# High parts of the differences one step behind their sums, and early differences in scratch in the order of use

## The chip, the cores and the metric

The kernel runs on one core of a Trainium2 chip. The metric is the device time of one execution in microseconds, as the median of several runs. The engines are TensorE (PE in the profile; PEld is its weight load), VectorE (DVE), ScalarE (ACT), GpSimdE (POOL) and SyncE (SP), which here only issues DMAs. Each engine takes its instructions in the order of the program and waits at an instruction until what it needs is there.

## The reference

```python
x = A_x                                   # 1 x 2048 x 640
xn = layernorm(x)
# A: 32 heads of 20, each position attends to 8 positions at distance 0, 2, ..., 14 behind it
q, k, v = split(xn @ wqkv)
o = sum_w softmax_w(q . k[s - 2w] * scale) * v[s - 2w]
s = o @ wo
# B: bilinear GLU, F = 1536
g = silu(((xn @ w_gate) * (xn @ w_up)) @ w_down)
out = x + s * g
```

## The kernel before

All products run on TensorE in a form that splits each fp32 operand into a high and a low part and takes three products (high x high, high x low, low x high): `ALL3`. A high part is a ScalarE copy into the float32r type, a low part is the GpSimdE or VectorE difference of the raw value and the high part.

The normalised, transposed input `xT` lies in SBUF in four chunks of 512 positions (buffers `xc`), each with high and low parts. The gate and up products of the GLU take two chunks at a time with a seven-product scheme (function `group`, line 1296 for its matmuls): of each pair of chunks it needs, beside the blocks themselves, the differences T1, T2, T3, T4 for two rows k = 0, 1 of the blocks. For the first pair of chunks (0 and 1) they are made early (`early_sums`, `early_high`), stored to a scratch in HBM, `t_scr`, of 12 units of 128 x 512, and loaded again by `load_t(n)`, three units at a time, into four SBUF tiles: load 0 is issued near the end of the qkv stage, loads 1 to 3 in the first `group` of the second pair. All are issued on GpSimdE's queue (line 1152). `T2_UNIT` gives the place of each difference in the scratch. For the second pair (chunks 2 and 3) the generator `differences(k)` makes them in SBUF while the qkv products run: `sums` is one GpSimdE addition or subtraction (line 1166), `parts` is one ScalarE copy (high part, line 1170) and one GpSimdE subtraction (low part, line 1171). T4 is kept raw until `last_difference`.

The order on each engine is the order in which the code issues. In the qkv stage (the loop over m and t from line 1360 on) each step issues one product of fifteen matmuls (`qkv`, line 435), its ScalarE copy out of PSUM (line 449), a DMA of every second copy to HBM scratch (line 453), a piece of attention (`advance`; lines 497 to 579, with GpSimdE's sums in line 515), at some steps a split of the next weights (lines 115 and 117), and, by a rate, one step of `differences`. So `yield` in `differences` is where other work comes between.

The PSUM banks of the qkv products in this stage are taken in turn: `ring[:] = [q_one, "g", "u"]`, where `q_one` is a single bank, and g and u have two each. In `group`, the seven products are issued in this order, which the names in the change refer to:

```python
W_IN = ("B11", "T1", "T2", "B22", "T3", "B21", "T4")
for n, j in enumerate((0, 5, 2, 1, 4, 3, 6)):
    y = b["ACACABA"[j]]
    runs = [(w_unit(f, H_IN[j], k)[i], x_in(W_IN[j], l, k, c0)) for i, l in ALL3 for k in range(2)]
```

So the order of use is B11, B21, T2, T1, T3, B22, T4, and within each first the high parts of k = 0, 1 and then the low parts.

Of the kernel before, what the change touches and what calls it, by code (L numbers as in the profile page):

```python
# [56 lines left out]
def kernel(  # L57
# [25 lines left out]
    def st(shape, tag, bufs, dt=F32):  # L83
        cnt[0] += 1
        pool = sb
        if tag == "gh":
            pool, bufs = gh_pool
        return pool.tile(shape, dt, tag=tag, bufs=bufs, name=f"{tag}_{cnt[0]}")
# [523 lines left out]
    def early_high(k):  # L612

        r0, r1, a, b = early_t[:4]
        for n, (j, y) in enumerate((("T1", a), ("T2", b), ("T3", r0), ("T4", r1))):
# [3 lines left out]
            for l, t in enumerate((early_t[4 + n], y)):  # L619
                nc.sync.dma_start(t_scr[:, T2_UNIT[j, l] + k] if j != "T4" else e_scr[l][:, k], t)  # L620

    T2_UNIT = {(j, a): 2 * n for n, (j, a) in enumerate((j, a) for j in ("T1", "T2", "T3") for a in range(2))}

    def advance(budget):
        credit[0] += budget
# [514 lines left out]
    def t_unit(j, a, k, c0=2):  # L1140

        if j == "T4":
            return xT[c0 + 1][a][:, k, :]
        n, i = T_UNIT[j, a, k] if c0 else divmod(T2_UNIT[j, a] + k, 3)
        while len(tt[c0]) <= n:
            tt[c0].append(slot([P, 3, CH]))
        return tt[c0][n][:, i]
# [12 lines left out]
    def differences(k):  # L1160

        def x(ch, a, m):
            return xT[ch][a][:, 2 * m + k, :].bitcast(F32)

        def sums(out, u, v, eng=nc.gpsimd.tensor_sub):
            eng(out, u, v)
            yield

        def parts(j, y):
            nc.scalar.activation(t_unit(j, 0, k), y, AF.Copy)  # L1170
            nc.gpsimd.tensor_sub(t_unit(j, 1, k), y, t_unit(j, 0, k).bitcast(F32))
            yield

        r0, a = st([P, CH], "gh", 5), st([P, CH], "gh", 5)
        yield from sums(r0, x(3, 0, 0), x(3, 1, 0), nc.gpsimd.tensor_add)
        yield from sums(a, r0, x(2, 0, 0))
        yield from sums(a, a, x(2, 1, 0))
        yield from parts("T1", a)
        r1 = st([P, CH], "gh", 5)
        yield from sums(r1, x(3, 0, 1), x(3, 1, 1), nc.gpsimd.tensor_add)  # L1180
        yield from sums(r0, r1, r0)
        yield from parts("T3", r0)
        yield from sums(r1, r1, a)
        yield from parts("T2", r1)
        z = t4[k] = st([P, CH], "gh", 5)
        yield from sums(z, x(2, 0, 1), r1)
        yield from sums(z, z, x(2, 1, 1), nc.gpsimd.tensor_add)

    def last_difference(k):
# [158 lines left out]
    def first_parts():  # L1348
# [4 lines left out]
        yield  # L1353

    steps += [differences(k) for k in range(2)]
    paced = 0.0
    last, BLOCK = len(MADE) - 1, (3, 4, 6, 8, 10)
    W_SUMS = ((1, 12), (2, 4), (2, 12), (3, 7))
    RATE = ((1.0, 0.4), (0.3, 0.2), (0.4, 0.6), (0.8, 0.8))
    for m, t in ((m, t) for m in range(1, len(MADE)) for t in range(DIL)):  # L1360
# [3 lines left out]
        for i in range(NE):  # L1364
            n = t * NE + i
# [185 lines left out]
    for m in range(n_prod):  # L1551
        n, j = divmod(m, 7)
# [82 lines left out]
```

## Time and profile before

| | |
|---|---|
| median of 3 runs | 739.09 us (739.0 to 740.01) |
| the profiled execution | 737.8 us, its span 736.0 us |
| granted TensorE clock | 1.000 |
| VectorE busy | 626.7 us (85%) |
| GpSimdE busy | 451.2 us (61%) |
| DMA | 143.78 MB, mean 195 GB/s |

The span runs from the first to the last instruction; the rest of the execution lies around it. The granted clock is that of the whole span. The qkv stage of the changed generator runs from about 110 to 273 us, the first groups from 273 us on. VectorE and GpSimdE carry the attention from about 90 to 487 us. Idle time of an engine costs only where TensorE ends up waiting for it, so the waits of TensorE are what to look for in the profile.

### The profile page before, as it was taken

How to read it: one execution, taken by the hardware profiler on the slowest of the kernel's cores; microseconds unless marked ns; L12 is line 12 of the kernel's file. 1: busy time of each engine (PE TensorE's matmuls, PEld its weight loads, DVE VectorE, ACT ScalarE, POOL GpSimd, SP SyncE). 2: the span in 40 equal slices, each digit the busy share in tenths (PEclk: the TensorE clock that was granted, in tenths of full speed). 3: DMA queues.
4: the chain of work that ended last, by engine and by line, in shares of the span. 5: the costliest groups of instructions: out<-in, count | busy, mean ns of one | idle time of the engine just before them, and what ended most of it. 6: DMA issues, size and time to landing. Idle time of an engine off the chain costs nothing.

```text
span 736.0 us, 11051 instructions
## 1 busy us (share of the span) xinstructions
PE 727.6 (99%) x4028; PEld 665.1 (90%) x4028; DVE 626.7 (85%) x726; ACT 302.0 (41%) x561; POOL 451.2 (61%) x383
## 2 busy tenths in 40 slices
PE   8999999999999999999999999999999999999997
PEld 6989989988999997888888888888999999999997
DVE  7676998799796989899889999979899987777775
ACT  5668312323232322333233323335556664444442
POOL 6159919897779889897879969767644650000000
PEclk9999999999999999999999999999999999999999
DMA  8786582789766659453723542277768965555534
GB/s 317 284 261 222 212 284 89 231 258 252 194 192 163 219 202 324 141 168 99 220 79 106 181 137 73 71 223 186 200 207 251 310 239 193 193 193 194 194 108 143
DMA packets 106148, 143.78 MB, mean 195 GB/s; under 512 B 23048, under 2 KB 75524, under 8 KB 106094
## 3 DMA queue, kind: packets, MB, share of 16 engines
q1 hardware_dynamic: 88366, 121.13, 51.4%
q10 hardware_dynamic: 16000, 12.78, 5.4%
q0 software_dynamic: 1728, 9.18, 5.1%
q8 instruction: 31, 0.51, 0.3%
q14 instruction: 23, 0.19, 0.1%
HBM read 94.40 MB, written 55.67 MB: 204 GB/s over the span
## 4 chain that ended last, share of the span: by engine, by line
PE 85%; POOL 7%; DMA 4%; issue 2%; DVE 1%; ACT 1%; SPq 1%; ACTq 0%; POOLq 0%; DVEq 0%
PE g L1296 15%; PE u L1296 10%; PE q L435 9%; PE q L867 7%; PE u L435 7%; PE g L435 6%; PE u L867 6%; PE q L1296 5%; PE e L867 4%; PE q L997 4%; PE g L867 3%; PE u L997 2%; PE g L126 2%; POOL kv L609 2%; PE u L126 2%
## 5 line engine op out<-in xcount | busy, mean ns | idle before, releaser
L515 POOL TENSOR_TENSOR o<-o,t 128x960 f32<-128x960 f32 (+1 forms) x66 | 133.4, 2021 | 11.0 <-DVE t L509 9.7
L509 DVE TENSOR_TENSOR t<-e,kv 128x960 f32<-128x960 f32 (+1 forms) x96 | 99.5, 1037 | 20.0 <-POOL o L515 20.0
L543 DVE TENSOR_TENSOR t<-q,kv 128x1920 f32<-128x1920 f32 (+1 forms) x48 | 92.4, 1925 | 3.5 <-DMA kv<-qkv_scr 3.3
L550 DVE TENSOR_REDUCE lg<-t 128x96 f32<-128x1920 f32 (+1 forms) x48 | 92.2, 1921 | 0.2
L435 PE MATMUL q<-s,xc 128*128 128x360 f32 (+1 forms) x465 | 85.9, 335 | 2.1 <-ACT s L449 1.1
L435 PEld LDWEIGHTS q<-s,xc 128*128 128x128 f32 x465 | 77.6, 188 | 6.5 <-ACT s L449 1.4
L117 POOL TENSOR_TENSOR s<-wraw,s 128x384 fp32r<-128x384 f32 (+6 forms) x57 | 68.4, 1218 | 21.2 <-ACT s L115 21.1
L1265 ACT ACTIVATE gh<-g 128x512 f32<-128x512 f32 x57 | 34.1, 598 | 110.4 <-PE g L1296 110.3
L435 PE MATMUL u<-s,xc 128*128 128x360 f32 (+1 forms) x375 | 68.4, 333 | 0.0
L435 PEld LDWEIGHTS u<-s,xc 128*128 128x128 f32 x375 | 62.7, 188 | 2.3
L435 PE MATMUL g<-s,xc 128*128 128x360 f32 (+1 forms) x330 | 60.6, 335 | 0.0
L1296 PE MATMUL g<-s,s 128*128 128x512 f32 x228 | 58.1, 390 | 0.5 <-DMA s<-t_scr 0.5
L1296 PE MATMUL u<-xc,s 128*128 128x512 f32 x228 | 57.8, 389 | 0.0
L435 PEld LDWEIGHTS g<-s,xc 128*128 128x128 f32 x330 | 55.3, 188 | 2.3
L1296 PEld LDWEIGHTS g<-s,s 128*128 128x128 f32 x228 | 42.7, 188 | 9.8 <-DMA s<-t_scr 1.0
L1296 PEld LDWEIGHTS u<-xc,s 128*128 128x128 f32 x228 | 42.8, 188 | 8.9
L867 PE MATMUL q<-xc,s 128*128 128x320 f32 x285 | 46.3, 309 | 0.0
L115 ACT ACTIVATE s<-wraw 128x384 fp32r<-128x384 f32 (+6 forms) x58 | 32.8, 581 | 31.7 <-PE g L1296 10.2
L867 PEld LDWEIGHTS q<-xc,s 128*128 128x128 f32 x285 | 43.0, 188 | 0.0
L1296 PE MATMUL q<-xc,pk 128*128 128x512 f32 x171 | 41.8, 389 | 0.0
L1296 PE MATMUL g<-xc,s 128*128 128x512 f32 x171 | 41.8, 389 | 0.0
L515 POOL TENSOR_TENSOR o<-t 128x960 f32<-128x960 f32 (+1 forms) x11 | 22.1, 2012 | 27.7 <-DVE t L509 26.1
(327 smaller groups left out, 1565.8 us busy)
## 6 DMA issues: line engine op xcount, KB each, us to landing
h_scr<-gh SPq DMA_DIRECT2D x48, 256.0 KB, 2.7
wraw<-in_wgu SPq DMA_DIRECT2D x11, 640.0 KB, 4.7
kv<-qkv_scr SPq DMA_DIRECT2D x14, 480.0 KB, 6.6
t<-h_scr SPq DMA_DIRECT2D x8, 768.0 KB, 6.0
qkv_scr<-s ACTq DMA_DIRECT2D x17, 360.0 KB, 4.6
kv<-qkv_scr SPq DMA_DIRECT2D x14, 367.5 KB, 6.9
s_scr<-gh SPq DMA_DIRECT2D x16, 320.0 KB, 3.6
gh<-s_scr SPq DMA_DIRECT2D x16, 320.0 KB, 3.7
```

Of the source, the lines that this page charges most:

```text
L115: nc.scalar.activation(hi, raw, AF.Copy)
L117: eng.tensor_sub(lo, raw, hi.bitcast(F32))
L126: nc.tensor.matmul(acc, a, b, start=first and n == 0, stop=last and n == len(runs) - 1)
L435: nc.tensor.matmul(p, xT[(r * NE + i) // TPC][a][:, k, t0:t0 + P], wq[m][b][k], start=n == 0, stop=n == len(runs) - 1, skip_group_check=ac ...
L509: nc.vector.tensor_mul(t.rearrange("p (n d) -> p n d", d=DH), e[:, :, w].unsqueeze(2).to_broadcast([P, NE * nh, DH]), v)
L515: return NE * c * cost, lambda: eng.tensor_add(y, z, t)
L543: nc.vector.tensor_mul(t, q, k)
L550: nc.vector.tensor_reduce(out=lg[:, :, j:j + 2].rearrange("p n a -> p a n"), in_=t.rearrange("p a (n d) -> p a n d", d=DH), op=ALU.add, ax ...
L867: nc.tensor.matmul(p, y[:, i, k], wd_part(name, k, l), start=new and r == 0, stop=r == len(runs) - 1, skip_group_check=True)
L997: nc.tensor.matmul(b, y, w, start=new and r == 0, stop=r == len(runs) - 1, skip_group_check=True)
L1265: nc.scalar.activation(kept[j], b["ACACABA"[j]], AF.Copy)
L1296: nc.tensor.matmul(y, w, x, start=j in (0, 1, 5) and r == 0, stop=r == len(runs) - 1, skip_group_check=True)
```

## The change

```diff
-    T2_UNIT = {(j, a): 2 * n for n, (j, a) in enumerate((j, a) for j in ("T1", "T2", "T3") for a in range(2))}
+    T2_UNIT = {(j, a): 2 * n for n, (j, a) in enumerate((j, a) for j in ("T2", "T1", "T3") for a in range(2))}
...
         yield from sums(a, a, x(2, 1, 0))
-        yield from parts("T1", a)
         r1 = st([P, CH], "gh", 5)
         yield from sums(r1, x(3, 0, 1), x(3, 1, 1), nc.gpsimd.tensor_add)
+        yield from parts("T1", a)
         yield from sums(r0, r1, r0)
+        yield from sums(r1, r1, a)
         yield from parts("T3", r0)
-        yield from sums(r1, r1, a)
-        yield from parts("T2", r1)
         z = t4[k] = st([P, CH], "gh", 5)
         yield from sums(z, x(2, 0, 1), r1)
+        yield from parts("T2", r1)
         yield from sums(z, z, x(2, 1, 1), nc.gpsimd.tensor_add)
```

In `differences` each `parts` now comes one `sums` later than before, so that another sum and one step of the other work stand between a sum and its high part. In the scratch, T2 takes units 0 to 3, T1 units 4 to 7 and T3 stays at 8 to 11. No instruction is added or taken away, and no tile changes size.

On ScalarE this is the place in the qkv stage, in the first round (k = 0), where the high parts of T1 (`gh_1177`) and T3 (`gh_1176`) are made (line 1170), among copies of products (449), their DMAs (453) and splits of weights (115):

```order
-L1170 ACTIVATE s_1248<-gh_1177 128x512
 L115 ACTIVATE s_1221<-wraw_1148 128x480
 L449 ACTIVATE pk_799<-q_1_68 128x3x120
+L1170 ACTIVATE s_1268<-gh_1177 128x512
 L449 ACTIVATE pk_799<-g_1273 128x3x120
 L453 DMA qkv_scr_1147<-pk_799 384x1x240
 L115 ACTIVATE s_1221<-wraw_1150 128x480
 L449 ACTIVATE s_798<-u_1297 128x3x120
-L1170 ACTIVATE s_1316<-gh_1176 128x512
 L449 ACTIVATE s_798<-q_1_68 128x3x120
 L453 DMA qkv_scr_1147<-s_798 384x1x240
+L1170 ACTIVATE s_1340<-gh_1176 128x512
```

Each of the two high parts has moved behind the next copy of a product in bank q (`q_1_68`); behind T3's there now follow a split and the copies of g and u.

GpSimdE at the same place: sums (1166), low parts (1171), low parts of weights (117) and the attention's sums (515). `gh_1176` is r0, `gh_1177` a, `gh_1248` (before: `gh_1269`) r1:

```order
-L1171 TENSOR_TENSOR s_1248<-gh_1177,s_1248 128x512
+L1166 TENSOR_TENSOR gh_1248<-xc_774 128x512
 L117 TENSOR_TENSOR s_1223<-wraw_1148,s_1221 128x480
-L1166 TENSOR_TENSOR gh_1269<-xc_774 128x512
+L1171 TENSOR_TENSOR s_1268<-gh_1177,s_1268 128x512
 L515 TENSOR_TENSOR o_1108<-o_1108,t_942 128x960
-L1166 TENSOR_TENSOR gh_1176<-gh_1269,gh_1176 128x512
+L1166 TENSOR_TENSOR gh_1176<-gh_1248,gh_1176 128x512
 L117 TENSOR_TENSOR s_1223<-wraw_1150,s_1221 128x480
 L515 TENSOR_TENSOR o_1108<-o_1108,t_942 128x960
-L1171 TENSOR_TENSOR s_1316<-gh_1176,s_1316 128x512
-L1166 TENSOR_TENSOR gh_1269<-gh_1269,gh_1177 128x512
```

The sum of r1 and the low part of T1 have changed places; the sum of T3 (`gh_1176<-`) stands where it stood, with the same instructions ahead of it.

TensorE in the first `group` of the first pair of chunks: `g_2746` is the product T2 and `u_2747` T1; `s_2544` is the tile of load 0, `s_2659` that of load 1, `s_2687` that of load 2:

```order
-L1296 MATMUL g_2746<-s_2659,s_2456 128x512 x2
-L1296 MATMUL g_2746<-s_2687,s_2456 128x512 x2
-L1296 MATMUL g_2746<-s_2659,s_2456 128x512 x2
-L1296 MATMUL u_2747<-s_2544,s_2456 128x512 x3
-L1296 MATMUL u_2747<-s_2659,s_2456 128x512
-L1296 MATMUL u_2747<-s_2544,s_2456 128x512 x2
+L1296 MATMUL g_2746<-s_2544,s_2456 128x512 x3
+L1296 MATMUL g_2746<-s_2659,s_2456 128x512
+L1296 MATMUL g_2746<-s_2544,s_2456 128x512 x2
+L1296 MATMUL u_2747<-s_2659,s_2456 128x512 x2
+L1296 MATMUL u_2747<-s_2687,s_2456 128x512 x2
+L1296 MATMUL u_2747<-s_2659,s_2456 128x512 x2
```

The product T2 read loads 1 and 2 and now reads loads 0 and 1; T1, the next, read loads 0 and 1 and now reads 1 and 2.

## The prediction

> **What bounds the kernel now.** I read the page first, then the waits of TensorE, then the timeline around each wait it names. Columns of a timeline row: start, busy time, engine, line, operation, output<-input, count; in brackets the idle time before it and what ended it.
>
> ```profile
> span 736.0 us, 11051 instructions
> PE 727.6 (99%) x4028; PEld 665.1 (90%) x4028; DVE 626.7 (85%) x726; ACT 302.0 (41%) x561; POOL 451.2 (61%) x383
> PE q L231 <- POOL lg masks.py:199: 1.4, 1, 1.4
> PE q L435 <- ACT s L449: 1.1, 1, 1.1
> PE q L435 <- DVE lg L276: 0.9, 1, 0.9
> PE g L1296 <- DMA s<-t_scr: 0.5, 1, 0.5
> ```
>
> TensorE sets the time: 8.4 us of the span are without a matmul. Its whole list of waits has four entries. The first and third belong to the start-up, which no row of the change touches; the other two are the places of this change. TensorE's own work is the same before and after: the same matmuls, two products reading other tiles. So at best those two waits go. All other engines count only where TensorE waits for them.
>
> **Wait A, ScalarE behind GpSimdE (first part of the change).**
>
> ```profile
> 121.50 2.56 PE L435 MATMUL q<-s,xc 128*128 128x360 f32 x15
> 126.30 2.56 PE L435 MATMUL u<-s,xc 128*128 128x360 f32 x15
> 127.59 1.29 POOL L1166 TENSOR_TENSOR gh<-gh,gh 128x512 f32<-128x512 f32 x1
> 128.92 0.63 ACT L1170 ACTIVATE s<-gh 128x512 fp32r<-128x512 f32 x1 [6.75 <-POOL gh L1166]
> 129.46 0.45 ACT L449 ACTIVATE s<-q 128x360 f32<-128x360 f32 x1
> 129.96 2.67 PE L435 MATMUL q<-s,xc 128*128 128x360 f32 x15 [1.10 <-ACT s L449]
> 131.02 0.46 ACT L449 ACTIVATE s<-g 128x360 f32<-128x360 f32 x1
> 132.47 2.56 PE L435 MATMUL g<-s,xc 128*128 128x360 f32 x15
> ```
>
> The q product that began at 121.50 was done at 124.06, but ScalarE copied it out only at 129.46: it had stood 6.75 us at the high part of T3, whose sum GpSimdE ended at 128.88. Bank q is single, so the next q product waited. Two groups of fifteen matmuls take 4.80 us start to start (121.50 to 126.30, so the g group between began at 123.90); from 126.30 to 132.47 two took 6.17. **A costs 1.37 us**, not the 1.10 of the wait alone: the first matmuls afterwards run without their weights loaded ahead.
>
> In the new ScalarE order the copy of q stands ahead of T3's high part, so it runs when its product is done, about 124.1, and q is free 4.6 us before 128.70. T3's sum still ends near 128.9: up to it GpSimdE has the same instructions, r1's sum and T1's low part having traded places. So the 6.75 us of standing stay, in part, on ScalarE; what stands behind them now are the copies of g (131.02) and then u. Banks g and u are double: g's next product, at 131.1, has the other bank, and the one held is wanted two g groups after the one that filled it, 2 x 7.2 us after 123.90, at 138.3. Cover: some 8 us. I cost it at nothing; if GpSimdE ran 8 us late it would be a stall again.
>
> The other moves. T1's high part now stands behind a copy of q instead of ahead of it, and T2's has three more ScalarE rows between it and its sum: neither waits longer. In the second round (k = 1) it is the other way about in one place:
>
> ```profile
> 196.14 1.29 POOL L1171 TENSOR_TENSOR s<-gh,s 128x512 fp32r<-128x512 f32 x1 [4.13 <-ACT s L1170]
> 203.07 0.56 DVE L577 TENSOR_REDUCE sm<-e 128x48 f32<-128x384 f32 x1 [5.95 <-ACT e L572]
> 203.87 0.47 ACT L449 ACTIVATE s<-q 128x360 f32<-128x360 f32 x1 [0.21 <-PE q L435]
> 208.43 0.97 POOL L117 TENSOR_TENSOR s<-wraw,s 128x360 fp32r<-128x360 f32 x1 [2.66 <-ACT s L115]
> 208.47 2.56 PE L435 MATMUL q<-s,xc 128*128 128x360 f32 x15
> ```
>
> T1's high part (0.63) now stands just ahead of this copy of q, which moves to about 204.3; q is wanted at 208.47, so 3.7 us cover it. Its low part (1.29) on GpSimdE moves from 196.14 to about 204.3; the attention sums behind 196.14 no longer wait 4.13 us, and by the weight split at 208.43, for which GpSimdE had stood 2.66 us, it is back in step. TensorE's list has no wait for a split. Bounds: 0, and 1.29 us if no gap took it up; I take 0.
>
> **Wait B, a product that waits for its scratch load (second part).**
>
> ```profile
> 278.84 1.65 POOL L1152 DMA_DIRECT2D s<-t_scr x3
> L1152 POOL DMA_DIRECT2D s<-t_scr x1: 583/583/583, 278.8 to 278.8; - x1
> DMA to landing us min/median/max: 8.6/8.6/8.6
> L1152 POOL DMA_DIRECT2D s<-t_scr x2: 537/540/544, 279.4 to 279.9; - x2
> DMA to landing us min/median/max: 10.6/11.2/11.9
> 288.69 0.41 PEld L1296 LDWEIGHTS g<-s,s 128*128 128x128 f32 x2
> 288.91 0.61 PE L1296 MATMUL g<-s,s 128*128 128x512 f32 x2
> 290.05 1.20 PE L1296 MATMUL g<-s,s 128*128 128x512 f32 x4 [0.53 <-DMA s<-t_scr]
> 291.09 1.54 PE L1296 MATMUL u<-s,s 128*128 128x512 f32 x6
> 292.47 0.84 PE L1296 MATMUL u<-xc,s 128*128 128x512 f32 x3
> 293.15 1.52 PE L1296 MATMUL g<-s,s 128*128 128x512 f32 x6
> ```
>
> The three loads landed at 287.4 (278.8 + 8.6), 290.0 (279.4 + 10.6) and 291.8 (279.9 + 11.9); the last two issues share a row, with the shortest and the longest time. The g product at 288.91 is T2; its third matmul reads a unit of the load that landed at 290.0. Six matmuls take 1.36 (three take 0.68, from 292.47 to 293.15); 288.91 to 291.09 took 2.18. **B costs 0.82 us.**
>
> After the change T2 reads the load issued long before and one unit of the load of 287.4, at its fourth matmul (weights at 288.69 + 0.68 = 289.37): 2 us of cover. What is late next is T1, the u product behind it. Its third matmul now takes the load of 290.0. Without B its weights start at 288.69 + 1.36 and the third's 0.45 later, at 290.50: 0.5 us of cover. T3 (at 293.15, then 292.33) takes the load of 291.8 at its second matmul, 0.23 on; less the 0.22 by which weights run ahead, 0.5 us of cover again. So B goes, with little to spare.
>
> **Do A and B add?** TensorE comes 1.37 us earlier to B. If the loads landed when they do now, T1 would be held at 290.0 in T2's place, six matmuls further: the two parts together would give 1.36 and not 2.19. So it matters whether the issue moves along.
>
> ```profile
> 268.67 0.47 ACT L449 ACTIVATE s<-q 128x360 f32<-128x360 f32 x1 [1.93 <-PE q L435]
> 269.74 0.74 ACT L115 ACTIVATE pk<-wraw 128x640 fp32r<-128x640 f32 x1 [0.60 <-ACT s L449]
> 270.55 1.57 POOL L117 TENSOR_TENSOR pk<-wraw,pk 128x640 fp32r<-128x640 f32 x1 [1.58 <-ACT pk L115]
> 272.08 4.88 POOL L515 TENSOR_TENSOR o<-o,t 128x640 f32<-128x640 f32 x3
> 276.91 2.00 POOL L117 TENSOR_TENSOR s<-wraw,s 128x384 fp32r<-128x384 f32 x2
> 380.13 0.56 DVE L577 TENSOR_REDUCE sm<-e 128x48 f32<-128x384 f32 x1 [2.51 <-ACT e L572]
> ```
>
> It does: from 270.55 to the issue at 278.84 GpSimdE has no gap, and at 270.55 it had stood 1.58 us for a ScalarE copy that itself stood for TensorE's q. If TensorE is 1.37 earlier, that start is too, and the loads with it. The attention on VectorE is tied to the same clock: at 203.07 it had stood 5.95 us, and at 380.13 2.51 us, for an exponential that queues on ScalarE behind copies of TensorE's banks. Both are longer than the gain up to there, so VectorE and GpSimdE come along and no cover behind 290 shrinks for good.
>
> Sum: 1.37 + 0.82 = 2.19 us. The profiled execution took 737.8 us, 1.8 around the span of 736.0; it would take 735.6. The runs shown have a median of 739.09, 1.3 above the profiled one; the gain comes off in full there: **736.9 us**, 0.30% less. A difference of 0.2%, 1.5 us, is about what a measurement of this kernel can tell from no change.
>
> A rule that speaks against B: the Trainium skill, DMA: Bandwidth & Descriptors, section "Two DMAs through the same engine are not ordered", says that nothing orders transfers across the 16 DMA engines, and that only the completion semaphore counts. By it a layout in order of use earns nothing for sure. The rows of this profile show the three loads landing in order of issue, 1.8 to 2.6 us apart; the sum by the rows stays 2.19, by the rule's worst case it is the third rival.
>
> **The rivals.**
> 1. *B is only handed on.* The issue stays where it is, or the loads land later by more than the cover of 0.5 us, and T1 waits instead of T2. The gain is 1.36 with loads at their old times: 737.7 us. For it: cover of half a microsecond, and loads of 8.6 to 11.9 us that share engines with others. Against: the chain above. Chance 0.18.
> 2. *A is only handed on.* Another copy behind T3's high part, or a bank, takes the stall's place, and only B is won, or less: 0 to 0.82, so about 738.3 to 739.1 us. For it: ScalarE still stands for GpSimdE. Against: 8 us of cover on g and u. Chance 0.08.
> 3. *Loads land out of order.* If the load of 287.4 were the last of the three, at 291.8, T2's fourth matmul would wait 2.4 us (291.8 - 289.37), or 3.8 with TensorE ahead by A's 1.37 and the loads not: against 2.19 gained, +0.2 to +1.6, that is 739.3 to 740.7 us. The rows speak against it. Chance 0.02. Only the rule of the Trainium skill above speaks for it.
> 4. *Slower: the loads collide.* The next unit's q and values are loaded right behind, on SyncE's queue.
>
> ```profile
> 288.04 1.29 SPq L1254 DMA_DIRECT2D h_scr<-gh  x2
> q<-qkv_scr SPq DMA_DIRECT2D x1, 480.0 KB, 8.4
> kv<-qkv_scr SPq DMA_DIRECT2D x1, 480.0 KB, 9.2
> DMA packets 1669, 4.12 MB, mean 349 GB/s; under 512 B 837, under 2 KB 837, under 8 KB 1667
> ```
>
> Between 278.3 and 290.1 the engines move 349 GB/s. If the 960 KB of these two came ahead of the scratch loads, the latter would land 2.8 us later; with their issue unshifted, 1.36 - 2.8 gives 1.4 us lost: 740.5 us. It is slower by over 0.2% from a delay of 2.8 us on (1.36 + 1.5), and from 1.4 slower at all. Against: they queue behind the stores of 288.04, which wait for TensorE's products and so cannot come earlier than it does. Chance 0.05.
>
> **How the numbers follow.** The forecast, both waits gone, 0.67 (735.9 to 737.5 with the spread of runs); rival 1 0.18, 2 0.08, 3 0.02, 4 0.05. The range runs from 735.8 (the forecast less a run's spread, as the profiled one lay 1.3 below the median) to 738.8, into rival 2's first half; left out are the rest of 2 and rivals 3 and 4 and some of the tails. Faster by over 0.2%: the forecast 0.62 (some of it is lost to the spread) and 0.08 of rival 1, whose 1.36 us lie just under the limit of 1.5: 0.70. Slower: 0.06. Within: 0.24.
>
> **What would show it.** After: the waits of TensorE have neither the entry of L435 for ScalarE nor that for t_scr; the q group after 126.30 starts near 128.70; ScalarE's L1170 still stands several microseconds near 128.9, with copies of g and u behind it; the T2 group lasts 1.36; PE's busy share rises with the busy time within some tenths of 727.6. Rival 1 shows as a wait of a u group for s<-t_scr; 2 as a wait of a g or u group for L449. I am wrong if TensorE waits at a place that has no entry now.

## The result, and the profile after

| | before | after |
|---|---|---|
| median, runs on the same chip | 739.71 us (6 runs, 739.0 to 740.26) | 735.44 us (6 runs, 735.2 to 735.61) |
| ratio, 95% interval | | 0.9943 [0.9931, 0.9956] |
| profiled execution / its span | 737.8 / 736.0 us | 735.6 / 733.8 us |

The changed kernel is 0.57% faster, about twice the 0.30% forecast, and its median lies 0.36 us below the lower end of the range. The two profiled executions, on the other hand, differ by 2.2 us, which is the forecast 2.19.

The head of the page after (span; busy time and share of each engine), then the waits of TensorE (engine, bank, line, what was waited for: us in total, times, longest):

```profile
span 733.8 us, 11050 instructions
PE 727.1 (99%) x4028; PEld 665.4 (91%) x4028; DVE 625.9 (85%) x726; ACT 302.7 (41%) x561; POOL 450.6 (61%) x383
```

```profile
PE q L231 <- POOL lg masks.py:199: 1.4, 1, 1.4
PE q L435 <- DVE lg L276: 1.0, 1, 1.0
```

Both waits of this change are gone; what is left are the two of the start-up. The timeline after, at the place of wait A (TensorE first, then ScalarE; columns as in the prediction):

```profile
126.31 2.56 PE L435 MATMUL u<-s,xc 128*128 128x360 f32 x15
128.71 2.56 PE L435 MATMUL q<-s,xc 128*128 128x360 f32 x15
124.11 0.47 ACT L449 ACTIVATE s<-q 128x360 f32<-128x360 f32 x1 [1.93 <-PE q L435]
128.61 0.63 ACT L1170 ACTIVATE s<-gh 128x512 fp32r<-128x512 f32 x1 [4.03 <-POOL gh L1166]
129.64 0.45 ACT L449 ACTIVATE s<-g 128x360 f32<-128x360 f32 x1
129.99 0.46 ACT L449 ACTIVATE s<-u 128x360 f32<-128x360 f32 x1
```

The copy of q runs at 124.11, when its product is done, and the next q product starts 2.40 us behind the u group, with no wait. ScalarE still stands 4.03 us for GpSimdE's sum of T3; only the copies of g and u are behind it now.

The place of wait B, GpSimdE's issue of the loads, TensorE, its weight loads, and the time from issue to landing of the three loads (in order of issue they took 8.1, 10.1 and 11.4 us):

```profile
277.46 1.64 POOL L1152 DMA_DIRECT2D s<-t_scr  x3
287.55 1.52 PE L1296 MATMUL g<-s,s 128*128 128x512 f32 x6
288.91 1.52 PE L1296 MATMUL u<-s,s 128*128 128x512 f32 x6
288.68 1.32 PEld L1296 LDWEIGHTS u<-s,s 128*128 128x128 f32 x6
DMA to landing us min/median/max: 8.1/10.1/11.4
```

T2 takes 1.36 us (287.55 to 288.91), not 2.18, and T1 behind it does not wait. The issue came 1.38 us earlier (278.84 before).

So everything that the prediction looked for in the trace is there. What it did not foresee must lie in the executions that were not profiled, since the runs of before have a median 1.9 us above the profiled 737.8, while those of after lie within 0.4 us of their profiled 735.6.

### The profile page after: what moved, and what is told of

Its sections match the earlier page's. It is cut to its first block, busy times and chain, and to the rows that moved or that the text cites. A ratio compares the mean times of both kernels' runs of the same rounds, so it can differ in the third digit from the quotient of the medians.

```text
span 733.8 us, 11050 instructions
## 1 busy us (share of the span) xinstructions
PE 727.1 (99%) x4028; PEld 665.4 (91%) x4028; DVE 625.9 (85%) x726; ACT 302.7 (41%) x561; POOL 450.6 (61%) x383
## 4 chain that ended last, share of the span: by engine, by line
PE 98%; DMA 1%; DVE 0%; SPq 0%; ACT 0%; issue 0%
PE g L1296 16%; PE q L435 11%; PE u L1296 11%; PE u L435 9%; PE g L435 8%; PE q L867 7%; PE u L867 6%; PE q L1296 5%; PE u L126 5%; PE g L126 5%; PE e L867 4%; PE q L997 4%; PE g L867 3%; PE u L997 2%; PE g L997 1%; PE e L997 1%
## 5 line engine op out<-in xcount | busy, mean ns | idle before, releaser
L515 POOL TENSOR_TENSOR o<-o,t 128x960 f32<-128x960 f32 (+1 forms) x66 | 133.5, 2023 | 11.6 <-DVE t L509 10.6
```

Of the source, the lines that this page charges most:

```text
L515: return NE * c * cost, lambda: eng.tensor_add(y, z, t)
```

## The experiments

Theory V (as it stood after the result): the profiled execution of before was an unusually quick one, and most executions of before lose some 2 us more, in a wait that varies. Rivals: the stall itself varies; the second round (k = 1) or the layout gains what was costed at nothing.

**The kernel before, unchanged, profiled again.**

> The kernel before, unchanged, profiled and timed once more. The timed gain is 4.3 us (739.71 to 735.44), the gain between the two profiled executions 2.2 us of span (736.0 to 733.8). Theory V (the profiled execution of before was a short one, and a wait that varies from run to run costs its other executions some 2 us more): a second profile has a span of 737 to 738.5 us, and the extra time stands at wait A (ScalarE's L1170 for the sum of T3) or at wait B (T2 for the scratch load). Rival P (profiling itself shortens this kernel by 2 us): the span is again 736.0 +- 0.3 with the same two waits of 1.1 and 0.5 us, while the timed runs are at 739 to 740.

Measured: 739.31 us (737.01 to 740.7, 11 runs), ratio 1.0004 [0.9992, 1.0017]; the profiled execution took 738.95 us. The page's head and TensorE's waits in it:

```profile
span 737.1 us, 11051 instructions
PE 730.0 (99%) x4028; PEld 667.6 (91%) x4028; DVE 624.6 (85%) x726; ACT 302.2 (41%) x561; POOL 450.6 (61%) x383
```

```profile
PE q L435 <- ACT s L449: 0.9, 1, 0.9
PE q L435 <- DVE lg L276: 0.3, 1, 0.3
```

The span is 3.3 us longer than after's, yet the waits explain 0.9 of it (and the start-up one is shorter): TensorE is *busy* 2.9 us longer with the same 4028 matmuls. Rival P, by which the span and both waits come out the same again, falls. Theory V is right that the first execution was a quick one, but wrong about the place: neither wait has grown. The timeline of TensorE shows where, in this execution of before:

```profile
125.91 2.56 PE L435 MATMUL u<-s,xc 128*128 128x360 f32 x15
129.37 2.74 PE L435 MATMUL q<-s,xc 128*128 128x360 f32 x15 [0.90 <-ACT s L449]
131.95 2.63 PE L435 MATMUL g<-s,xc 128*128 128x360 f32 x15
134.41 2.63 PE L435 MATMUL u<-s,xc 128*128 128x360 f32 x15
262.90 2.63 PE L435 MATMUL g<-s,xc 128*128 128x360 f32 x15
265.37 0.82 PE L435 MATMUL u<-s,xc 128*128 128x360 f32 x4
290.93 1.52 PE L1296 MATMUL g<-s,s 128*128 128x512 f32 x6
```

Behind wait A a group of fifteen takes 2.47 us start to start (262.90 to 265.37) in place of 2.40, and stays so until the stage ends. By matmul, of those of line 435 that ran between 196 and 262 us, after and then this execution (min/median/max of the duration of one, ns; a matmul starts before the one ahead of it has ended):

```profile
L435 PE MATMUL g<-s,xc x145: 322/322/322, 195.7 to 262.0; 128*128 128x360 f32 x145
```

```profile
L435 PE MATMUL g<-s,xc x135: 325/327/329, 196.3 to 257.8; 128*128 128x360 f32 x135
```

From start to start these are 160.00 and 164.45 ns apart on average. The 569 matmuls of 360 columns behind the stall, at 4.45 ns each, make 2.53 us; the 480-column ones between them hardly move (216.67 and 216.74), and of the 512-column ones behind them the first ten are up to 236 ns apart and the rest 226.67, as after the change; that is 0.05 us in all. The granted clock is no part of it:

```profile
196.00:262.00 66.00, 66.00 (x403) 1.00 0.65 190
```

(window, its length, TensorE busy and matmuls, granted clock, DMA share, GB/s). The execution of before profiled first had the same stall and 160.00 ns behind it.

And wait B is missing here: the second load landed 9.7 us after its issue (10.6 in the first profile), just before T2's third matmul asked for it. From the u group at 125.91 to T2 at 290.93 there are 165.02 us; after the change, from 126.31 to 287.55, 161.24. Of these 3.78 us, 1.06 are the stall (3.46 in place of 2.40), 0.1 the first matmuls behind it, and 2.6 the pace.

**The two parts alone.** Before with only the new order of `differences`, and before with only the new layout of the scratch (first line of the diff):

```diff
-        yield from parts("T1", a)
...
+        yield from parts("T1", a)
         yield from sums(r0, r1, r0)
-        yield from parts("T3", r0)
         yield from sums(r1, r1, a)
-        yield from parts("T2", r1)
+        yield from parts("T3", r0)
...
+        yield from parts("T2", r1)
```

> Only the order in differences(k); the scratch layout as before. Theory VA (the varying wait is A, set by how late GpSimdE reaches T3's sum): the gain is all but B's 0.8 us, ratio 0.9954 or so, 736.0 to 736.6 us, and the runs lie within 0.5 us of each other. Theory VB (the varying wait is B): only A's 1.4 us are won, about 738.3 us, and the runs scatter as those of before do.

> Only the layout T2, T1, T3 in scratch; differences(k) as before. Theory VA: B's 0.8 us are won, or less, as T1 may meet its load instead: 738.9 to 739.7 us, and the runs scatter as those of before do. Theory VB: 2.9 us are won, about 736.8 us, with little scatter.

Measured: order alone 735.85 us (735.46 to 736.31, 5 runs), ratio 0.9956 [0.9942, 0.9969]; layout alone 739.49 us (736.54 to 740.98, 11 runs), ratio 0.9994 [0.9981, 1.0006]. The timeline of TensorE, order alone and then layout alone:

```profile
126.18 2.56 PE L435 MATMUL u<-s,xc 128*128 128x360 f32 x15
128.58 2.56 PE L435 MATMUL q<-s,xc 128*128 128x360 f32 x15
```

```profile
129.82 2.74 PE L435 MATMUL q<-s,xc 128*128 128x360 f32 x15 [1.01 <-ACT s L449]
132.39 2.63 PE L435 MATMUL g<-s,xc 128*128 128x360 f32 x15
```

The order takes the whole gain: no stall, no slow pace. Its 735.85 us lie below the 736.0 to 736.6 that theory VA expected with B left in; in its profiled execution B is absent too, with nothing to spare: the second load landed at 287.6 and T2's third weights went in at about the same time (287.20 for the first, 0.44 more for the third). The layout alone leaves stall and pace as they were and gains nothing that can be measured by the medians. In its profiled execution it did spare a wait: the second load took 10.7 us and landed at 292.35, and with the old layout T2 would have asked for it at 291.58 (weights from 291.13, the third 0.45 later). So B seems to come when that load takes long (10.6 and 10.7 us in two of these profiles, 9.7 in the two without the new layout that show no wait for it). With the order the layout may still buy what margin B lacks, 0 to 0.4 us by the medians, which the intervals do not separate.

**The second round left in the old order.** The changed kernel, with each `parts` of k = 1 back behind its own sum:

```diff
+        if k:
+            yield from parts("T1", a)
...
-        yield from parts("T1", a)
+        if not k:
+            yield from parts("T1", a)
         yield from sums(r0, r1, r0)
+        if k:
+            yield from parts("T3", r0)
         yield from sums(r1, r1, a)
-        yield from parts("T3", r0)
+        yield from parts("T2" if k else "T3", r1 if k else r0)
...
-        yield from parts("T2", r1)
+        if not k:
+            yield from parts("T2", r1)
```

> The changed kernel with the old order in the second round (k = 1) of differences. If all of A lies in the first round, it is as fast as the change, ratio 0.994 to before, 735.4 us. Rival: the second round's stand of GpSimdE (4.13 us behind L1170) or its high part of T2 ahead of a copy of bank q carries part of the gain: 736 to 737.5 us, with a wait of TensorE for ScalarE near 203 or 226 us.

Measured: 735.99 us (735.24 to 736.72, 5 runs), ratio 0.9956 [0.9943, 0.9968]. The moves of the second round gain and cost nothing that can be seen: the median lies at the edge of the rival's 736 to 737.5, but the trace has no wait of TensorE in the qkv stage, which the rival needs. (Its profiled execution, 736.72, started about 1.1 us late, at a granted clock of 0.88 over the first 14 us where after's had 1.00; the profiled execution with the stop of 0.95 us, below, started as late, and such starts make part of the scatter.)

**A stop put into the changed kernel.** If the slow pace comes from the stop and not from the old order, a stop of another origin must bring it back. The copy of bank q at one step is repeated, which changes no result and makes TensorE wait for the bank:

```diff
-            nc.scalar.activation(y[...], p[...], AF.Copy)
+            for _ in range(N if (m, r, i) == PLACE else 1):
+                nc.scalar.activation(y[...], p[...], AF.Copy)
```

First with N = 17, at three places: where before stalled (1, 0, 7), late in the stage (4, 1, 1), and in a unit with 480 columns (2, 0, 3); and the changed kernel beside them.

> The changed kernel, in which ScalarE writes the copy of one product of bank q 17 times instead of once (the same values), the product at whose successor wait A stood, so that TensorE stands there for some 1 us again. Theory S (a break in the row of 360-column matmuls can leave them at 164.45 ns instead of 160.00 until the end of the qkv stage, and that is what the timed runs of before lose beside the wait): the time rises by the break plus 2.2 to 2.5 us in most runs, 738.5 to 740 us, with a few runs 2.4 us below the others, and the profile shows 360-column matmuls 164 to 165 ns apart behind the break. Rival O (the slow pace comes from the old order of the sums, not from the break): the time rises by the break alone, to 736.5 to 737.2 us, and the matmuls stay 160 ns apart.

> The same break, made at the first product of bank q in the last part of the qkv stage (near 239 us; TensorE stands near 243 us). Theory S: the break plus at most 0.8 us (some 180 matmuls of 360 columns are left, by 4.45 ns): 737 to 738 us. Rival O: the break alone.

> The same break in the part with products of 480 columns (near 156 us). Theory S, if the pace outlasts the 480-column part, as it did in two profiles: the break plus about 2.1 us (some 465 matmuls of 360 columns from 196 us on, by 4.45 ns), and 480-column matmuls as before. If a break among 480-column matmuls does not set the pace: the break alone, 736.5 to 737.5 us.

> The changed kernel unchanged, on the chip of the three above: 735.2 to 735.8 us, all matmuls of 360 columns 160 ns apart. Beside the kernel with the order alone (735.85 us on another chip) it says what the layout is worth: 0 to 0.5 us.

Measured: 743.67 us (741.13 to 745.02), 742.94 (741.67 to 743.72, 5 runs; a sixth, of 808.24 us at a mean granted clock of 0.846, is left out and nothing here explains it) and 743.16 (741.45 to 745.39), 6 runs each of the first and the third; the changed kernel 735.58 (735.29 to 736.46, 5 runs), ratio 0.9952 [0.9937, 0.9967]. The stops were sized badly: 3.8 us, not about 1. The timeline and the windows of the first:

```profile
126.17 2.56 PE L435 MATMUL u<-s,xc 128*128 128x360 f32 x15
132.54 4.18 PE L435 MATMUL q<-s,xc 128*128 128x360 f32 x15 [3.81 <-ACT s L450]
136.56 1.60 PE L435 MATMUL g<-s,xc 128*128 128x360 f32 x9
```

```profile
132.50:135.50 3.00, 2.96 (x10) 0.50 0.36 126
```

Behind a stop of 3.81 us the granted clock was 0.50 for some 3 us, and nine matmuls ran at 300 ns: 3.97 us for the stop (6.37 in place of 2.40) and 1.62 for the group behind it (4.02), 5.6 in all, which with 735.5 gives the 741.13 of this execution; its later matmuls ran at 160.00. The Trainium skill, TensorE: Matmul & The Clock Gate, section "What's actually happening", has the clock halved after an idle window of about 3.4 us; these three runs agree, and the shorter stops below (granted clock 1.00 right behind them) do too. Three of the other five runs lie 2.1 to 2.6 us above the profiled one, as the pace would have it, and two 3.7 to 3.9, but the halved clock is a second cost that neither theory had counted, so the times of these three kernels decide nothing. The trace of the late stop does say something:

```profile
246.72 4.26 PE L435 MATMUL q<-s,xc 128*128 128x360 f32 x15 [3.82 <-ACT s L450]
253.29 2.63 PE L435 MATMUL u<-s,xc 128*128 128x360 f32 x15
255.76 2.63 PE L435 MATMUL q<-s,xc 128*128 128x360 f32 x15
```

Here, with the new order of the sums, the groups behind the stop took 2.47 us (253.29 to 255.76) until the stage ended, which rival O excludes. In the traces of the other two kernels they took 2.40.

**The same with a short stop.** N = 11 at the first place, 11 at the late one, 12 at the 480-column one, then 10 at the first place.

> The changed kernel, with the copy of bank q made 11 times in place of once at the place where the kernel before stalled first (second chunk pair, first row, step 7), so that TensorE waits there about 1 us and no more; the times of the copies before this one (17 copies) came out as a wait of 3.8 us, long enough to lower the clock for 2.7 us, which this run avoids. Theory (a wait of about 1 us leaves the 360-column matmuls behind it at 164.45 ns instead of 160.00 until the stage ends, whatever caused the wait): 735.5 + about 1.0 for the wait + 2.2 to 2.5 for some 500 to 550 matmuls at 4.45 ns = 738.7 to 739.1 in most executions, with a few about 2.4 lower, and 164 to 165 ns between those matmuls in the slow ones. Rival (the slower pace belongs to the old order of the sums): the wait alone, 736.3 to 737.0, and 160.00 ns throughout.

> The same with 11 copies, late in the stage (fifth chunk pair, second row, step 1), where some 100 to 180 of the 360-column matmuls are still to come. Theory: 735.5 + about 1.0 + 0.4 to 0.8 = 736.9 to 737.3, so about 1.8 us below the run with the wait at the first place. Rival (old order): the wait alone, 736.3 to 737.0, the same as at the first place.

> The same with 12 copies in a unit whose matmuls have 480 columns (third chunk pair, first row, step 3). Theory, if the slower pace is carried over to the 360-column matmuls that come later: 735.5 + about 1.0 + 1.5 to 2.1 = 738.0 to 738.6. If the 480-column matmuls end it: 736.5 to 736.9, as the rival (old order) also has it: so this run tells only what the pace needs, given the first.

> The wait at the first place (second chunk pair, first row, step 7) cut by one copy, 10 in place of 11: the copies stand 0.50 us apart, so the stop of 0.95 us becomes about 0.45 us. If any stop of TensorE leaves the 360-column matmuls at 164.45 ns: 735.5 + 0.45 + 2.2 to 2.5 = 738.2 to 738.5 in most executions. If it needs a longer stop: the stop alone, 735.9 to 736.2 (up to 737 where the start of the program comes 1.1 us later, as in some executions of every kernel here).

| stop at | stop | median, 12 runs | ratio to before |
|---|---|---|---|
| first place, N = 11 | 0.95 us | 739.43 (736.96 to 740.53) | 1.0001 [0.9989, 1.0014] |
| late in the stage | 0.96 us | 737.43 (736.22 to 738.7) | 0.9977 [0.9965, 0.999] |
| 480 columns | 0.96 us | 738.93 (736.74 to 740.18) | 0.999 [0.9978, 1.0001] |
| first place, N = 10 | 0.45 us | 738.57 (735.94 to 738.93) | 0.9983 [0.9974, 0.9993] |

The stop is how much later than its neighbours' spacing the first matmul behind it starts. TensorE's timeline with N = 11, then with N = 10, at the first place:

```profile
127.37 2.56 PE L435 MATMUL u<-s,xc 128*128 128x360 f32 x15
130.72 2.74 PE L435 MATMUL q<-s,xc 128*128 128x360 f32 x15 [0.79 <-ACT s L450]
133.29 2.63 PE L435 MATMUL g<-s,xc 128*128 128x360 f32 x15
135.76 2.63 PE L435 MATMUL u<-s,xc 128*128 128x360 f32 x15
```

```profile
126.03 2.56 PE L435 MATMUL u<-s,xc 128*128 128x360 f32 x15
128.88 2.74 PE L435 MATMUL q<-s,xc 128*128 128x360 f32 x15 [0.29 <-ACT s L450]
131.46 2.63 PE L435 MATMUL g<-s,xc 128*128 128x360 f32 x15
```

In both, groups behind the stop take 2.47 us, to the end of the stage, in a kernel whose sums stand in the new order. In the traces the stage, from its first 360-column matmul (near 105 us) to the first 512-column one behind it, lasts 167.20 us in the changed kernel without a stop, 170.82 with the stop of 0.95 and 170.32 with the stop of 0.45. So half the stop still costs 3.1 us: 0.45 for itself and some 2.6 for the pace. (By the medians the two differ by 0.9 and not 0.5: the profiled run of the first, 740.39 us, started 1.1 us late, and four more of its runs took as long.) The stop alone would have given 736.3 to 737.0 and 735.9 to 736.2, and falls. All four medians lie 0.1 to 0.3 us above the ranges of the theory. The late stop:

```profile
240.66 2.56 PE L435 MATMUL u<-s,xc 128*128 128x360 f32 x15
244.02 2.74 PE L435 MATMUL q<-s,xc 128*128 128x360 f32 x15 [0.79 <-ACT s L450]
246.59 2.63 PE L435 MATMUL g<-s,xc 128*128 128x360 f32 x15
```

Fewer matmuls are left there, and it costs 1.9 us: 1.07 at the stop and 0.8 for the pace (the stage lasts 169.07). The stop among 480 columns was caught in an execution of the quick kind (736.79), and shows what the others lack:

```profile
159.38 3.42 PE L435 MATMUL u<-s,xc 128*128 128x480 f32 x15
163.59 3.53 PE L435 MATMUL q<-s,xc 128*128 128x480 f32 x15 [0.80 <-ACT s L450]
201.02 2.56 PE L435 MATMUL q<-s,xc 128*128 128x360 f32 x15
203.42 2.56 PE L435 MATMUL g<-s,xc 128*128 128x360 f32 x15
```

Here the 360-column groups behind stayed at 2.40. Three of its 12 runs lie at 736.74 to 736.86, where the stop alone puts them (735.5 + 1.07 = 736.6), and the other nine 1.9 to 3.4 us above, with no run between. That the pace was slow in those nine is inferred from their times; none of them was profiled.

## Why the prediction was right in the trace and wrong in the median

- *"TensorE's own work is the same before and after ... So at best those two waits go."* This is where the prediction went wrong. The matmuls are the same, but not the time that they take: in the second profile of before TensorE is busy 730.0 us, after the change 727.1. What that did to the forecast stands at the median below.
- *Wait A, 1.37 us; the copy of q ahead of T3's high part frees the bank.* Right: the q group started at 128.71 (forecast near 128.70), and g and u covered the rest of the standing.
- *Wait B, 0.82 us.* Right for the profiled execution: T2 took 1.36. Cover measured for T1: its third weights at 289.13 (288.68 + 0.45) against a landing at about 288.1, 1.0 us where 0.5 was forecast, since the load took 10.1 and not 10.6. But B does not come in every execution: in the second profile of before it is absent, and the layout alone gained nothing by the median.
- *The issue moves along with TensorE by 1.37.* Right: 1.38. With it rival 1 (B handed on) falls.
- *The second round costs nothing; attention falls back into step.* Right: GpSimdE stood 6.41 us for T1's low part, which began at 202.92 (forecast about 204.3), and ahead of 206.56 it stood again, 1.41 us for a load; the kernel with the second round in the old order came out the same.
- *Rival 2 (A handed on), rival 3 (loads out of order), rival 4 (loads collide).* None came: no new wait on TensorE, and the loads landed in order in this profile too, 8.1, 10.1 and 11.4 us after their issues; the rule of the Trainium skill, DMA: Bandwidth & Descriptors, section "Two DMAs through the same engine are not ordered", that nothing orders them across the engines was not put to the test by any run.
- *The sum 2.19, profiled execution 737.8 to 735.6.* Right, to 0.1 us.
- *"The gain comes off in full there", at the median of 739.09: 736.9.* This is the step of the sum that failed, and it rests on the premise in the first point. It took the 1.3 us between the profiled execution and the median for scatter that both kernels share. It is not: in most executions of before, the matmuls behind wait A run at 164.45 ns in place of 160.00, 2.6 us in all, and go away with the wait. The term missing from the sum is this pace. The sum for such an execution is 1.17 for the stall (1.06, and 0.1 behind it) + 2.6 for the pace + 0 for B = 3.8 us; measured, 3.78 between the same two groups of the two traces, and 3.6 to 4.3 between the medians of three comparisons (739.71, 739.41 and 739.45 of before against 735.44, 735.58 and the order alone's 735.85 give 4.3, 3.8 and 3.6).

How often: of the 94 timed runs of the kernel before, 9 lie at 736.3 to 737.8 us and 85 at 738.7 and above, with none between. That the pace is what parts them is inferred from the times: one execution of each kind was profiled. The profiled execution of the prediction was of the rarer kind. There was a sign of it ahead of the result: its 737.8 lay below every one of the three times shown (739.0 to 740.01), and in its start-up matmuls of the same shape stood 164 ns apart (last section), though those of the stage ran at one pace throughout. A prediction from it alone could at best have held the 1.3 us open.

Open: what decides, at a stop, which pace follows (with stops of 0.45 and 0.95 us at the first place, 2 runs of 12 each kept the quick one, judged by their times); and why 360-column matmuls keep it, 480-column ones hardly show it and 512-column ones lose it. The traces show the slower spacing, not its cause.

## What to carry to other kernels

Before a gain is carried from one profiled execution to a median, compare the two: an execution below all the timed ones may be of another kind, and the difference may be a cost that the change also removes. A stop of a busy TensorE may not be over when its wait ends; compare the start-to-start time of groups of the same shape ahead of it and behind it, because a slower pace is booked as busy time and no list of waits names it. So removing a short stop early in a long run of matmuls can be worth more than its length: here 0.45 us cost 3.1.

## What the runs showed of the hardware that was not expected

- A stop of 0.45 to 1.1 us left the 128x360 matmuls at 164.45 ns start to start in place of 160.00 for the rest of a stage (up to 569 of them over 145 us), across a stretch of 480-column ones in between, at a granted clock of 1.00, in most executions and not in all.
- It does not take a listed wait, nor the old order of the sums. The start-up of the changed kernel, from its profile (L126 makes other products, of 256 and 512 columns):

```profile
18.65 5.18 PE L435 MATMUL q<-s,xc 128*128 128x360 f32 x30
23.67 1.95 PE L126 MATMUL g<-xc,s 128*128 128x256 f32 x15
30.95 3.56 PE L126 MATMUL u<-xc,s 128*128 128x512 f32 x15
34.35 4.96 PE L435 MATMUL q<-s,xc 128*128 128x360 f32 x30
39.15 2.56 PE L435 MATMUL e<-s,xc 128*128 128x360 f32 x15
```

  The thirty at 18.65 take 5.02 us (to 23.67), 163 to 167 ns each behind a first step of 246; no wait is listed ahead of them. The thirty at 34.35 take 4.80 (to 39.15), 160 each. All fourteen profiles show these two spacings at these two places. Between them stand thirty matmuls of 256 columns and thirty of 512.
- At the end of the qkv stage, behind slow 360-column matmuls, the first three to ten of 512 columns are up to 236 ns apart, and from then on 226.67. So the pace seems to end among 512-column matmuls; that these alone end it was not tried.
- A stop of 3.8 us halved the granted clock for about 3 us: nine matmuls of 360 columns at 300 ns, with 480 columns seven at 400 ns.
